# First feed-forward layer of an attention and MLP kernel: a second Strassen level for two of the seven products, by pairs of steps

## The chip, the cores and the metric

The kernel runs on one core of one Trainium2 chip. The metric is the device time of one execution in microseconds (us). Three runs of the kernel before gave 872.02, 872.38 and 872.67; the median is 872.38.

The engines are called as the profile calls them: PE (TensorE) multiplies matrices and writes to PSUM, which has eight banks of 128x512 float32; PEld is PE's loading of weights; DVE (VectorE), ACT (ScalarE) and POOL (GpSimd) work elementwise; SP (SyncE) issues the DMAs.

## The reference

Attention in which a query sees only the keys of its own hash bucket, then an MLP with a fast GELU, all in float32 (the weights of the MLP come as float64):

```python
q_bits = (np.einsum('bhsd,dk->bhsk', q, proj) > 0)          # 6 bits a row, the bucket
mask = q_bucket[:, :, :, None] == k_bucket[:, :, None, :]
attn = softmax(where(mask, q @ k.T / 8, -1e9)); x = attn @ v # B, H, S, D = 4, 8, 768, 64
h = x @ w_in                                                 # x: 3072 x 512, w_in: 512 x 2048
g = h * (1.0 / (1.0 + np.exp(-1.702 * h)))
out = g @ w_out                                              # w_out: 2048 x 512
```

## The kernel before

**Stages.** Attention goes over 16 pairs of heads and leaves `xT`, x transposed, in SBUF (to 316 us of the profile). `feed_forward` (line 695) computes h in a first layer (316.6 to 606.2 us) and out in a second (to 866). Both layers use Strassen's scheme in Winograd's form: a product of two matrices, each cut into 2x2 quarters, is made with seven products of quarters or of sums of quarters, in place of eight. `sums_a` (line 208) makes the four sums of a left matrix, `sums_b` (line 216) those of a right one. The dictionaries `LEFT` and `RIGHT` say which quarter or sum each of the products 1 to 7 takes.

**The first layer.** It has 24 steps, numbered 0 to 23: three blocks of 1024 tokens (`sb`), eight pieces of w_in's columns (`mt`) in each. A step is one call of `hidden` (line 731): seven products of 128x512, each two matmuls over the inner dimension (`product`, line 716). A product goes to a PSUM bank; products 6, 7 and 4 are added up in the bank of product 1 (`start=False`), product 3 in that of product 5. ACT copies the bank between them to `u`, `v` and `c22` in SBUF (lines 726, 746, 750), DVE adds the bank of product 5 to c22 (line 751), product 2 to u (line 755), product 3's bank to v (line 764), ACT applies the GELU in place (line 741). So a step ends with four quarters of g. POOL then makes the sums of these quarters that the second layer wants (lines 219 to 222, "POOL's four" below), and SP stores quarters and sums in DRAM (line 738). The first product of the next step stands ahead of products 4 and 3 (`head`).

**What else runs in the first layer.** The order on PE, DVE, ACT and POOL is the order in which the program is written (`ORDERED`, line 18, under `tc.manual_schedule`); SP's order is the scheduler's. At the ends of the steps DVE gets, from the dictionary `todo` (lines 917 to 929):

- the conversions of w_out's 16 chunks and of the last two of w_in from float64 (`convert`, line 158: lines 180, 182, 188, 193, 195 and 198 on DVE, line 190 on ACT, line 162 the DMA of the chunk `raw`), one chunk in a step, with one buffer for `raw`; none in steps 0, 7 and 15;
- the four x sums of the next token block (`sums_b` on 128x1024) in steps 7 and 15: three before products 4 and 3, one after;
- sums of w_out (`low` from step 17, `high` in step 21), and sums of g at the end.

POOL gets the sums of w_in for the next step in the first eight steps (`in_sums`, line 236), later some of w_out (`inner_sums`). When step 0 has been written, attention writes its last part: `invert` and `norm` (lines 488 and 504) divide the last heads by their sums, on DVE. In step 21 the pool of the conversions is closed, and `fetch(0)` (line 802) brings the first quarter of g for the second layer.

**PSUM.** Six banks for the products, two for the conversions (`part`, `size`). The tiles u, v, c12, c21 and c22 have two buffers each.

Of the kernel before, what the change touches and what calls it, by code (L numbers as in the profile page):

```python
# [19 lines left out]
P = 128  # L20
# [18 lines left out]
def kernel(  # L39
# [168 lines left out]
    def sums_a(eng, a11, a12, s3, a22, s1, s2, s4, a21=None):  # L208

        a21 = s3 if a21 is None else a21  # L210
        return [lambda: eng.tensor_tensor(s1, a21, a22, op=Alu.add),
                lambda: eng.tensor_tensor(s3, a11, a21, op=Alu.subtract),
                lambda: eng.tensor_tensor(s2, s1, a11, op=Alu.subtract),
                lambda: eng.tensor_tensor(s4, a12, s2, op=Alu.subtract)]

    def sums_b(eng, b11, b12, b21, b22, t1, t2, t4):


        return [lambda: eng.tensor_tensor(t1, b12, b11, op=Alu.subtract),  # L219
                lambda: eng.tensor_tensor(b12, b22, b12, op=Alu.subtract),  # L220
                lambda: eng.tensor_tensor(t2, b22, t1, op=Alu.subtract),  # L221
                lambda: eng.tensor_tensor(t4, b21, t2, op=Alu.subtract)]
# [4 lines left out]
    def quarters_in(cols):  # L227
        w = [w_in_sb[:, K2 * k : K2 * (k + 1), F2 * i + cols.start : F2 * i + cols.stop]
             for i in range(2) for k in range(2)]
        return w + [s_in[:, i, :, cols] for i in range(3)]  # L230
# [2 lines left out]
        x = [xT[:, K2 * k : K2 * (k + 1), (2 * sb + j) * XT : (2 * sb + j + 1) * XT] for k in range(2) for j in range(2)]  # L233
        return x + [t_x[:, i] for i in range(3)]

    def in_sums(mt):
        return sums_a(nc.gpsimd, *quarters_in(slice(mt * P, (mt + 1) * P)))


    def load(ld, n, v_bufs=2):  # L240
# [454 lines left out]
    def feed_forward(tag, late=()):  # L695
# [9 lines left out]
        with ExitStack() as fctx:  # L705
            stage_ctx = fctx.enter_context(ExitStack())
            stage = stage_ctx.enter_context(tc.tile_pool(name=f"stage{tag}", bufs=2, side="right"))
            late = list(late)
            sets = [fctx.enter_context(tc.tile_pool(name=f"f0{tag}", bufs=6, space=PSUM, side="right"))]
            todo, turn = {}, [-1]  # L710

            def bank():
                turn[0] += 1
                return sets[turn[0] % 8 // 6 if len(sets) > 1 else 0].tile([P, XT], F32, tag="p", name="product")

            def product(ps, sb, mt, i, start=True):
                wq, xq = quarters_in(slice(mt * P, (mt + 1) * P)), quarters_x(sb)
                for kc in range(K2):
                    nc.tensor.matmul(ps, wq[LEFT[i]][:, kc, :], xq[RIGHT[i]][:, kc, :],  # L719
                                     start=(start and kc == 0), stop=(kc == K2 - 1), skip_group_check=not start)  # L720

            def head(n):

                ps, u = bank(), stage.tile([P, XT], F32, tag="u", name="u")
                product(ps, *divmod(n, FC // 2), 1)
                nc.scalar.copy(u, ps)  # L726
                return ps, u

            heads = {}

            def hidden(sb, mt, mid=(), end=()):
                n = sb * (FC // 2) + mt
                a, u = heads.pop(n) if n in heads else head(n)
                v, c12, c21, c22 = (stage.tile([P, XT], F32, tag=x, name=x) for x in ("v", "c12", "c21", "c22"))
                t2, t4 = (stage.tile([P, XT], F32, tag=x, name=x, bufs=1) for x in ("t2", "t4"))

                def keep(at, x):
                    loader[0].dma_start(out=g_dram[len(LEFT) * sb + at, :, mt, :], in_=x)

                def emit(c, at=None, of=None):  # L740
                    nc.scalar.activation(c, c if of is None else of, Act.Gelu_apprx_sigmoid)  # L741
                    if at is not None:
                        keep(at, c)

                product(a, sb, mt, 6, False)
                nc.scalar.copy(v, a)
                b = bank()
                product(b, sb, mt, 5)
                product(a, sb, mt, 7, False)
                nc.scalar.copy(c22, a)  # L750
                nc.vector.tensor_tensor(c22, b, c22, op=Alu.add)
                emit(c22, 3)
                c = bank()
                product(c, sb, mt, 2)
                nc.vector.tensor_tensor(u, c, u, op=Alu.add)
                emit(u, 0)
                if n + 1 < n1 * (FC // 2):
                    heads[n + 1] = head(n + 1)
                for x in mid:
                    x()  # L760
                product(a, sb, mt, 4, False)
                emit(c21, 2, a)
                product(b, sb, mt, 3, False)
                nc.vector.tensor_tensor(c12, b, v, op=Alu.add)  # L764
                emit(c12)

                for f, kept in zip(sums_b(nc.gpsimd, u, c12, c21, c22, v, t2, t4), ((4, v), (1, c12), (5, t2), (6, t4))):
                    f()
                    keep(*kept)
                for x in end:  # L770
                    x()

# [29 lines left out]
            def fetch(n):  # L802
                sb, o = steps_out[n]
                for h in range(2):
                    cs = slice(h * F4, (h + 1) * F4)
                    loader[0].dma_start(out=raw_g[n % 2][:, cs], in_=g_dram[len(LEFT) * sb + RIGHT[o], :, cs, :])
# [90 lines left out]
                            yield  # L897
                    yield

            MT = FC // 2  # L900
            for sb in range(n1):
                for mt in range(MT):
                    n = sb * MT + mt
                    if n == 1:
                        wop = fctx.enter_context(tc.tile_pool(name=f"wo{tag}", bufs=1))
                        cv_ctx = fctx.enter_context(ExitStack())
                        cv = cv_ctx.enter_context(tc.tile_pool(name=f"cv{tag}", bufs=1))
                        cps = cv_ctx.enter_context(tc.tile_pool(name=f"cps{tag}", bufs=1, space=PSUM))


                        w_out_sb = wop.tile([P, 4, FC, P], F32, name="w_out_sb")
                        wqs += [w_out_sb[:, 2 * i : 2 * i + 2, MT * k : MT * (k + 1), :] for i in range(2) for k in range(2)]
                        wqs += [xT[:, i, 0 : 4 * XT].rearrange("p (h c d) -> p h c d", h=2, d=P) for i in range(3)]

                        order = [8 * k + 4 * c + i for c in range(2) for k in range(2) for i in range(4)]
                        chunks = [(w_out_sb[:, :, fc, :].rearrange("p r x -> p x r"), wo[fc]) for fc in order]
                        steps = conversions(cv, cps, late + chunks)
                        free = [i for i in range(LATE + 1, 3 * MT) if i % MT != MT - 1]
                        for i in (list(range(1, LATE + 1)) if late else []) + free[:FC]:
                            todo[i] = [lambda: next(steps)] * 2  # L920
                        low, high = (sums_a(nc.vector, *(x[:, :, F4 * c : F4 * (c + 1), :] for x in wqs)) for c in range(2))
                        first = 2 * MT + 1
                        for i, f in enumerate(low):
                            todo[first + i] = todo[first + i] + [f]
                        todo[first + 1] = todo[first + 1] + inner_sums(0)[:2]
                        todo[first + 2] = todo[first + 2] + inner_sums(0)[2:]
                        todo[first + 4] = high + inner_sums(1)
                        todo[first + 5] = inner_sums(2)
                        todo[first + 6] = inner_sums(3)
                    if n == 3 * MT - 3:  # L930
                        cv_ctx.close()
                        sets.append(fctx.enter_context(tc.tile_pool(name=f"f1{tag}", bufs=2, space=PSUM)))
                        turn[0] = 7
                        gp = fctx.enter_context(tc.tile_pool(name=f"gp{tag}", bufs=1))
                        raw_g[0] = gp.tile([P, FC // 2, XT], F32, name="raw_g")
                        fetch(0)
                    if sb == 0 and mt + 1 < MT:
                        for f in in_sums(mt + 1):
                            f()
                    x = sums_b(nc.vector, *quarters_x(sb + 1)) if mt == MT - 1 and sb + 1 < n1 else []  # L940
                    t = {3 * MT - 2: g_sums(0)[:2], 3 * MT - 1: g_sums(0)[2:]}.get(n, []) if n > 3 * MT - 3 else []
                    hidden(sb, mt, x[:3] + ([lambda: fetch(1)] if n == 3 * MT - 1 else []), x[3:] + t + todo.pop(n, []))
                    yield
            stage_ctx.close()
            st2 = fctx.enter_context(tc.tile_pool(name=f"st2{tag}", bufs=1, side="right"))
            ys.update({j: st2.tile([P, XT // 32, P], F32, name=f"y{j}") for j in range(2)})
# [105 lines left out]
```

## Time and profile before

| | |
|---|---|
| median of 3 runs | 872.38 us |
| the profiled execution | 872.87 us |
| its span, first to last instruction | 871.0 us |
| mean granted TensorE clock | 0.997 |
| PE, DVE, POOL busy in 316.6 to 606.2 | 288.79, 171.58, 156.61 us of 289.6 |
| the same in 606.2 to 866 | 254.40, 213.24, 38.02 us of 259.8 |

A row of the profile's groups names the line, the engine, the operation, the tile written and those read, the shape and the count; after the bar come the busy time in us, the mean of one in ns, and the idle time of the engine before them with what ended it. A row of the timeline has the start in us, the duration (of the whole run of instructions, where "x3" says that three are merged), engine, line, operation, and in brackets the idle time before it. A row of the waits has the waiting instruction, what released it, the us in total, how many times, and the longest. A float32 matmul leaves two records in the trace.

### The profile page before, as it was taken

The numbers are of one execution on the slowest core, as the hardware profiler recorded it, in microseconds if no ns is written. First come the engines' busy times: TensorE is split into PE (matmuls) and PEld (weight loads), VectorE is DVE, ScalarE is ACT, GpSimd is POOL, SyncE is SP. The second block draws the span as 40 slices with busy tenths as digits, with TensorE's granted clock in tenths as the row PEclk, the third lists the DMA queues.
The fourth block names the chain that finished last, engine by engine and source line by source line (L and its number), as shares of the span: only waits on it lengthen the run. The fifth ranks groups of instructions, "written<-read, shape, count | busy, mean of one in ns | idle before, by whom it ended". The sixth has DMA issues, their size and how long they took to land.

```text
span 871.0 us, 13350 instructions
## 1 busy us (share of the span) xinstructions
PE 857.9 (99%) x4845; PEld 499.2 (57%) x4845; DVE 661.4 (76%) x924; ACT 340.2 (39%) x567; POOL 311.6 (36%) x275
## 2 busy tenths in 40 slices
PE   9999999999999999999999999999999999999996
PEld 5444444444444444444444444445878888888885
DVE  4589999999999875457555556676788977897786
ACT  5866667776666643434334333433000000000000
POOL 4242234333223465665443344559903100000000
PEclk9999999999999999999999999999999999999998
DMA  5636645456652104665456655576744675467524
GB/s 127 96 57 109 104 84 85 84 99 117 99 97 61 56 2 157 205 208 181 172 198 197 217 181 172 190 254 223 271 156 158 199 243 201 163 209 243 194 97 99
DMA packets 169161, 132.09 MB, mean 152 GB/s; under 512 B 123616, under 2 KB 138112, under 8 KB 163712
## 3 DMA queue, kind: packets, MB, share of 16 engines
q1 hardware_dynamic: 166528, 129.70, 52.5%
q10 hardware_dynamic: 2560, 1.46, 0.8%
q8 instruction: 40, 0.66, 0.3%
q14 instruction: 33, 0.27, 0.1%
HBM read 79.69 MB, written 50.33 MB: 149 GB/s over the span
## 4 chain that ended last, share of the span: by engine, by line
PE 95%; DVE 3%; issue 0%; DMA 0%; ACT 0%; ACTq 0%; DVEq 0%
PE product L719 33%; PE product L851 26%; PE ps L432 18%; PE av L465 15%; DVE xT L855 1%; PE dn L486 1%; PE hash L408 1%; PE tp L366 1%; DVE y L831 1%; DMA k<-in_k_dram 0%; DVE v L855 0%; PE hash L373 0%; DVE t2a L221 0%; DVE raw_g L220 0%; ACTq L838 0%
## 5 line engine op out<-in xcount | busy, mean ns | idle before, releaser
L433 ACT ACTIVATE e<-ps 128x768 f32<-128x768 f32 x192 | 151.2, 812 | 25.7 <-PE ps L432 23.2
L432 PE MATMUL ps<-qT,kT 64*128 64x384 f32 x768 | 155.1, 482 | 0.0
L465 PE MATMUL av<-e,v 128*32 128x385 f32 x1536 | 128.0, 487 | 0.0
L719 PE MATMUL product<-xT,w_in_sb 128*128 128x512 f32 x288 | 127.8, 592 | 0.0
L440 POOL TENSOR_TENSOR acc<-e 128x768 f32<-128x768 f32 x32 | 51.7, 1617 | 194.4 <-ACT e L433 175.0
L719 PEld LDWEIGHTS product<-xT,w_in_sb 128*128 128x128 f32 x288 | 54.6, 190 | 69.0 <-issue 68.5
L465 PEld LDWEIGHTS av<-e,v 128*32 128x32 f32 x1536 | 48.6, 109 | 76.2 <-issue 74.9
L432 PEld LDWEIGHTS ps<-qT,kT 64*128 64x128 f32 x768 | 68.0, 187 | 38.5 <-issue 38.4
L719 PE MATMUL product<-t_x,s_in 128*128 128x512 f32 x192 | 86.4, 592 | 0.8 <-ACT u L726 0.8
L764 DVE TENSOR_TENSOR c<-product,v 128x512 f32<-128x512 f32 x24 | 16.6, 690 | 90.8 <-PE product L719 90.8
L219 POOL TENSOR_TENSOR v<-c,u 128x512 f32<-128x512 f32 x24 | 32.3, 1345 | 128.1 <-ACT c L741 128.1
L864 ACT COPY u<-product 128x256 f32<-128x256 f32 x21 | 7.8, 372 | 174.1 <-PE product L851 140.9
L719 PEld LDWEIGHTS product<-t_x,s_in 128*128 128x128 f32 x192 | 36.4, 190 | 47.1 <-issue 45.2
L432 PE MATMUL ps<-qf,kf 64*128 64x384 bf16 x384 | 62.9, 324 | 0.1
L741 ACT ACTIVATE c<-c 128x512 f32<-128x512 f32 x48 | 30.3, 630 | 72.3 <-DVE c L764 43.7
L441 POOL TENSOR_TENSOR acc<-acc,e 128x768 f32<-128x768 f32 x32 | 55.8, 1745 | 2.5
L446 DVE SCALAR_TENSOR_TENSOR acc<-e 128x768 f32<-128x768 f32 x32 | 47.7, 1489 | 5.1 <-ACT e L433 5.1
L719 PE MATMUL product<-t_x,w_in_sb 128*128 128x512 f32 x96 | 45.1, 592 | 0.0
L719 PE MATMUL product<-xT,s_in 128*128 128x512 f32 x96 | 45.1, 592 | 0.0
L750 ACT COPY c<-product 128x512 f32<-128x512 f32 x24 | 14.1, 586 | 66.3 <-PE product L719 66.3
L432 PEld LDWEIGHTS <-kf 64*128 64x128 bf16 x384 | 18.9, 94 | 35.1 <-issue 6.2
L448 DVE TENSOR_TENSOR acc<-acc,e 128x768 f32<-128x768 f32 x32 | 34.3, 1071 | 3.3
(206 smaller groups left out, 1513.4 us busy)
## 6 DMA issues: line engine op xcount, KB each, us to landing
raw_g<-g_dram SPq DMA_DIRECT2D x22, 1024.0 KB
s_in<-g_dram SPq DMA_DIRECT2D x20, 1024.0 KB
g_dram<-c SPq DMA_DIRECT2D x72, 256.0 KB
g_dram<-t SPq DMA_DIRECT2D x48, 256.0 KB
raw<-in_moe_w_in_dram SPq DMA_DIRECT2D x16, 512.0 KB
raw<-in_moe_w_out_dram SPq DMA_DIRECT2D x16, 512.0 KB
v<-in_v_dram SPq DMA_DIRECT2D x32, 192.0 KB
g_dram<-u SPq DMA_DIRECT2D x24, 256.0 KB
```

Of the source, the lines that this page charges most:

```text
L219: return [lambda: eng.tensor_tensor(t1, b12, b11, op=Alu.subtract), lambda: eng.tensor_tensor(b12, b22, b12, op=Alu.subtract), lambda: eng ...
L432: nc.tensor.matmul(ps[:, j, 0:HS], a[hs, keys], m[hs, cols], start=not last, stop=last)
L433: nc.scalar.activation(es[c][:, kt, :, 0:HS], ps[:, :, 0:HS], Act.Exp, scale=1.0 / D**0.5)
L440: nc.gpsimd.tensor_tensor(acc, es[c][:, 0, :, 0:HS], es[c][:, 1, :, 0:HS], op=Alu.add)
L441: nc.gpsimd.tensor_tensor(acc, acc, es[c][:, 2, :, 0:HS], op=Alu.add)
L446: nc.vector.scalar_tensor_tensor(acc, e[0], T * TINY, e[1], op0=Alu.add, op1=Alu.add)
L448: nc.vector.tensor_tensor(acc, acc, x, op=Alu.add)
L465: nc.tensor.matmul(av[D * j + d : D * j + d + 32, :], vt[:, t, j, d : d + 32], es[c][:, t, j, :], start=(t == 0), stop=(t == T - 1))
L719: nc.tensor.matmul(ps, wq[LEFT[i]][:, kc, :], xq[RIGHT[i]][:, kc, :], start=(start and kc == 0), stop=(kc == K2 - 1), skip_group_check=not ...
L741: nc.scalar.activation(c, c if of is None else of, Act.Gelu_apprx_sigmoid)
L764: nc.vector.tensor_tensor(c12, b, v, op=Alu.add)
L851: nc.tensor.matmul(ps, wq[LEFT[i]][:, c, :], gq[RIGHT[i]][:, c, :], start=(c == 0), stop=(c == F4 - 1))
```

## The change

Ten pairs of steps (numbered 0 to 9, steps 0 to 19) replace ten times two calls of `hidden`; steps 20 to 23 stay single. In a pair, product 2 over both steps, and product 3 over both, is seen as one product of a left matrix of 256x256 and a right one of 256x512, and is made with seven matmuls of 128x256 (`nested`) in place of eight column halves, which were four matmuls of 128x512. The seven go in six parts: part 1 is matmul 1, part 2 matmuls 6 and 2, parts 3 to 6 matmuls 7, 5, 4 and 3. Matmuls 1, 6, 7 and 4 are added up in one PSUM bank ("a"), 2, 5 and 3 go to another ("x"); the pool `inner` has one buffer of each. After each matmul DVE adds the bank so far to a 128x256 half of u or v. The parts of product 2 (S1 to S6 below) stand between the other products of the pair, those of product 3 (T1 to T6) behind the last one and between the products of the next pair (`behind`).

```python
def nested(o, sb, t, base, done):
    (q11, q12), (q21, q22) = ((x[:, 0:TH], x[:, TH:XT]) for x in base)
    ...
    def first():
        add(q11, go(1, "a"), q11)
    def second():
        add(q12, go(6), q12)
        add(q11, go(2, "x"), q11)
    def third():
        add(q22, go(7), q22)
    def fourth():
        add(q22, go(5, "x"), q22)
    def fifth():
        add(q21, go(4), q21)
        done(1)
    def sixth():
        add(q12, go(3), q12)
        done(0)
```

The order of a pair (`old()` is the next part of product 3 of the pair before; `hook(i)` is other work, put in below):

```python
p1(0); old(); hook(1); p1(1); old()
yield
hook(2); p6(0); old(); hook(3); p6(1); old(); hook(4); p5(0); old()
second = nested(2, sb, t, u, done2)
second[0](); hook(5); p7(0); corner(0); second[1](); hook(6); p7(1); second[2]()
hook(7); p5(1); corner(1); second[3](); hook(8); p4(0); second[4]()
hook(9); p4(1); second[5]()
third = nested(3, sb, t, v, done3)
third[0](); behind.extend(third[1:]); hook(10)
```

`p5` adds product 5's bank to v at once, `corner` adds it to c22. POOL's four, now for both steps, eight sums of 128x512, are written after T6 (`done3`). At the `yield` in pair 0 attention writes `invert` and `norm`; before, they came after the whole of step 0.

The nested products need sums of their own: `nest_w` makes eight of 128x128 on POOL for a pair's weights (pairs 0 to 3, kept for the later token blocks), `nest_x` eight of 128x256 on DVE for a token block (pairs 0, 4 and 8). The hooks:

```diff
+                if t == 0:
...
+                    more = nest_x(0, places[0])
+                    hooks[3] = more[2] + nest_w(0)
+                    hooks[4] = more[3]
...
+                if at == 0 and sb > 0:
+                    on(1, more[2])
+                    on(3, more[3][:2])
+                    on(4, more[3][2:])
+                x = todo.pop(2 * t, [])
+                on(2, x[0:1])
+                on(3, x[1:2])
+                on(5, x[2:])
+                x = todo.pop(2 * t + 1, [])
+                on(7, x[0:1])
+                on(9, x[1:2])
+                on(10, x[2:])
+                if t + 1 < MT // 2:
+                    on(5, in_sums(t + 1))
+                    on(8, nest_w(t + 1))
+                if at == MT // 2 - 1:
+                    x = sums_b(nc.vector, *quarters_x(sb + 1))
+                    more = nest_x(sb + 1, places[sb + 1])
+                    on(8, x[0:1])
+                    on(9, x[1:2])
+                    on(10, x[2:4])
```

So a chunk's conversion, before in one go at the end of a step, is cut in two: lines 180, 182 and 188 at hook 2 or 7, lines 193, 195 and 198 at hook 3 or 9. `in_sums` now makes the sums of two steps at once (128x2x256). The four x sums stand at hooks 8, 9 and 10 of pairs 3 and 7, the eight of `nest_x` in pairs 4 and 8 at hooks 1, 3 and 4.

Buffers: PSUM has four banks for the products of a pair, two for the nested ones, two for the conversions. u, v and c22 have four buffers and c21 three (two in the pool `stage`, the others in a pool `twice`, which lies where attention's small tiles were); t1, t2 and t4 have one. v is no longer overwritten by a sum; the sum has t1. In step 21 `twice` and `inner` are closed with the pool of the conversions, before `fetch(0)`.

## The prediction

> **What bounds the kernel now.** I read the page first: busy time, then the chain that ended last.
>
> ```profile
> PE 857.9 (99%) x4845; PEld 499.2 (57%) x4845; DVE 661.4 (76%) x924; ACT 340.2 (39%) x567; POOL 311.6 (36%) x275
> ...
> PE 95%; DVE 3%; issue 0%; DMA 0%; ACT 0%; ACTq 0%; DVEq 0%
> ```
>
> TensorE (PE) sets the time. The chain in order of time gives the rate of each stage.
>
> ```profile
> 319.38 286.92 PE product L719 x668
> ...
> 686.08 160.83 PE product L851 x744
> ```
>
> In the first layer (316.6 to 606.2 us) 668 records take 286.92 us, 429.5 ns each; a matmul of 128x512 leaves two records (672 for 336), so one product (two matmuls) takes 1.718 us. A record of 256 columns, each with weights of its own, takes 160.83/744 = 216.2 ns: a nested matmul takes 0.432 us. The waits, filtered to PE, show how little of the first layer is idle now.
>
> ```profile
> PE product L851 <- DVE t2a L221: 1.7, 1, 1.7
> ...
> PE product L719 <- ACT u L726: 0.8, 1, 0.8
> ```
>
> So nothing is won by moving work off other engines, only by fewer PE columns; and every new wait of PE is paid in full.
>
> **What is removed.** A product over two steps took 2 x 1.718 = 3.436 us; nested it takes 7 x 0.432 = 3.027. Twenty products save 20 x 0.409 = **8.2 us**. The first step's wait of 0.8 goes too, because two first products now stand there. What is late next is VectorE (DVE).
>
> **What DVE gets.** Its timeline in one step (start, duration):
>
> ```profile
> 403.78 0.69 DVE L764 TENSOR_TENSOR c<-product,v 128x512 f32<-128x512 f32 x1 [4.46 <-PE product L719]
> 404.38 0.68 DVE L180 TENSOR_SCALAR part<-raw 128x512 uint32<-128x512 uint32 x1
> 405.10 0.69 DVE L182 SCALAR_TENSOR_TENSOR bits<-raw,part 128x512 uint32<-128x512 uint32 x1
> 405.83 0.69 DVE L188 TENSOR_SCALAR part<-bits 128x512 uint32<-128x512 uint32 x1
> 406.55 0.70 DVE L193 SCALAR_TENSOR_TENSOR part<-raw,part 128x512 f32<-128x512 uint32 x1
> 407.29 1.05 DVE L195 TENSOR_TENSOR w_out_sb<-bits,part 128x512 f32<-128x512 f32 x1
> 408.44 1.05 DVE L198 SCALAR_TENSOR_TENSOR w_out_sb<-size,w_out_sb 128x512 f32<-128x512 f32 x1
> ```
>
> From start to start a 512 add costs 0.60; the first half of a conversion 2.1 (L180, L182, L188), the second 2.9 (L193, L195, L198). A 256 add from PSUM has a row of its own below, 0.41; pairs of them follow at 0.37. A nested pair gives DVE 14 x 0.37 + 4 x 0.60 + 2 x 5.0 = 17.6 us in 23.2 us of PE: it fits on average. But DVE is in order, and each nested chain has one PSUM bank: part 6 or 7 may not write until DVE has added the part before. On PE a pair runs p1, T2, p1, T3, p6, T4, p6, T5, p5, T6, S1, p7, S2, p7, S3, p5, S4, p4, S5, p4, S6, T1 (S: second product, T: third, of which five parts hang over into the next pair). S1 comes at 11.2 us of the pair and takes the bank that DVE empties with T5's add. DVE: T3's add ends at 5.4, half a conversion 7.5, T4's add 7.8, the other half 10.7, T5's add 11.1, and PE starts 0.15 after DVE (637.37 after 637.22 in the trace): 11.2. **The slack is zero**; whatever makes DVE later in the first half of a pair is paid by PE one to one. Behind a waiting S1 stand all later products. Four things make it later.
>
> *The start.* Now DVE normalises the last heads after the whole first step; the changed order puts that, and the eight sums of the x blocks (128x256), ahead of the first add.
>
> ```profile
> 332.29 0.57 DVE L492 STREAM_TRANSPOSE rt<-dn 128x384 f32<-128x384 f32 x1
> ...
> 335.20 1.33 DVE L506 TENSOR_TENSOR xT<-xT,rs 128x768 f32<-128x768 f32 x1
> ```
>
> That is 4.2 us. DVE is busy with L178 to L222 until 323.05, so norm ends at 327.3, eight sums at 0.45 (0.44 apart at 642.36, below) at 331.0, the first 512 add and S1's add at 332.1. PE reaches S2 after five products, S1 and p7: 316.6 + 8.6 + 0.4 + 1.7 = 327.3. Wait **5.0**. Low end 2.5 (L178 to L198 took 1.1 beside POOL, 0.69 elsewhere); high end 9, eight sums beside POOL at about 1.0:
>
> ```profile
> 627.52 1.07 DVE L855 TENSOR_TENSOR v<-v,xT 128x256 f32<-128x256 f32 x1
> ...
> 642.36 0.88 DVE L855 TENSOR_TENSOR xT<-xT 128x256 f32<-128x256 f32 x2
> ```
>
> I take 5.0, the nearer row. The first of these has POOL (GpSimd) busy beside it, the second not.
>
> *The turns of the x blocks (pairs 4 and 8).* Four sums of 128x1024 now fall at the end of pairs 3 and 7 and after T1; then eight of 128x256 in the next pair, before T5's add. At 1.22 each (411.25 to 416.4, POOL idle) S1 waits 1.9; all at 2.17 (598.53, POOL at 2.25 beside it) about 5.1. POOL's eight sums of a pair (1.35 us each) begin after T6 and last to the end of the pair, so about half meets them. I take **3.0 each, 6.0** (3.8 to 10.2).
>
> The Trainium skill (SBUF — State Buffer, "Who interferes with whom") states that a DVE instruction with two SBUF inputs contends with a GpSimd instruction that reads SBUF, one with at most one SBUF input does not. The trace agrees: L751 (one input in PSUM) stays at 0.69 beside L220 at 601.9. By that rule the nested adds stay at 0.41 and the x sums do not; the sum would be nearer the high end of the two terms above.
>
> *The loader.* A raw chunk has one buffer, and its DMA stands behind other stores on SP.
>
> ```profile
> 409.09 1.67 SPq L738 DMA_DIRECT2D g_dram<-t  x2
> 410.87 0.37 SPq L162 DMA_DIRECT2D raw<-in_moe_w_out_dram  x1
> ```
>
> In the changed order the chunk for a pair's first conversion is issued after POOL's last store of the pair before and three held-back stores, at about 1.6 us of the pair; DVE wants it at 5.4. At 339.48 such a DMA was issued, and L180 read at 344.30 without waiting: it takes at most 4.8, so it may be up to 1 us late, with three stores of 0.65 us ahead perhaps 1.5. Pairs 2, 3, 5, 6, 7, 9: 0 to 9 us; I take **2.7**.
>
> *The rest.* POOL's sums of w_in for the next pair follow its eight: p6 may wait 0.7 twice, I take 0.7 (0 to 3). Wide w_out sums of 2.1 us in pairs 8 and 9: 0.5 (0 to 2). In steps 20 to 23, single again, the c22 and v copies wait on ACT behind the last T parts: 1.0 (0 to 1.5).
>
> **Sum.** -8.2 - 0.8 + 5.0 + 6.0 + 2.7 + 0.7 + 0.5 + 1.0 = +6.9. The profiled execution took 872.87 (span 871.0), 0.5 over the median of the runs: 872.4 + 6.9 = about **879.5 us**. The ends: all low -2.7 (869.7), all high about +26.
>
> One row could overturn the gain itself; the row of the 256 adds stands below it.
>
> ```profile
> L851 PE MATMUL product<-raw_g,xT 128*128 128x256 f32 x152 | 35.1, 379 | 0.0
> ...
> L855 DVE TENSOR_TENSOR xT<-product,xT 128x256 f32<-128x256 f32 x45 | 17.4, 413 | 0.0
> ```
>
> The 379 is a record from start to modelled end. If it were its share of PE, nested parts would cost more than they replace; but 744 records in 160.83 us exclude that. The order of the changed kernel does show 140 small matmuls in place of 80 large ones, so it does what it says.
>
> **Rivals.**
> 1. *DVE keeps ahead; faster.* Place: S1 in each pair. If the chunk always lands before 5.4 us, the x sums miss POOL's and the start costs 2.5, waits come to 6.3 against 9.0 saved: 869.7, 869.5 as a round figure. It decides at waits of 9. For it: DVE's idle time now, 24% of the span. Against: the start alone is fixed by 4.2 us of norm. 0.13.
> 2. *It cancels*, waits of 7.5 to 11: 872.4. 0.10.
> 3. *The loader falls behind everywhere*: 9 in place of 2.7: 886, up to 893 with POOL contention. For it: every store now waits in SP behind POOL's eight. 0.15.
> 4. *The clock drops after the long waits.* The granted clock reads 1.00 over each of the two layers (stretches 316.6 to 606.2 and on to 866), which hold the waits of 0.8 and 1.7; a wait of 5 has no row. If half the clock were granted as long as the wait lasted, +2.5 at the start and about 1.3 in each of pairs 4 and 8: 884.5. 0.07. The Trainium skill (TensorE: Matmul & The Clock Gate, "What's actually happening") has the clock halved after an idle window of about 3.4 us; by that rule this rival acts at the start alone.
> 5. The forecast, 874.1 to 886: 0.55.
>
> **The numbers.** A measurement here tells about 0.2% (1.7 us) from no change. Faster 0.13 (rival 1), same 0.10 (rival 2), slower 0.55 + 0.15 + 0.07 = 0.77. The range 870.5 to 888 leaves out most of rival 1 and the upper half of rival 3, 0.2 together.
>
> **What would show it.** PE's waits in the first layer name DVE at the nested line: one of 4 to 6 us about 11 to 16 us after the first product, two of 2 to 4 us a third and two thirds on, and about 0.5 in other pairs. PE's busy time falls by about 8. L180 waits for a DMA if the loader term is real. Wrong if PE shows fewer than 9 us of waits, or if S2's first wait is under 2.5.

## The result, and the profile after

The changed kernel takes 891.94 us (median of 4 executions, 890.42 to 892.73) against 872.2 for the kernel before in the same comparison: ratio 1.0224, 95% interval 1.0206 to 1.0242. It is 19.7 us slower. The forecast was 7.1 us slower than 872.4, with a range up to 888.0: the direction was right, the size was not.

The page of the changed kernel, PE's and DVE's busy time and the shares of the chain that ended last:

```profile
PE 858.9 (97%) x4965; PEld 522.4 (59%) x4965; DVE 705.7 (79%) x1068; ACT 340.5 (38%) x567; POOL 324.5 (36%) x291
...
PE 74%; DVE 13%; POOL 4%; issue 4%; DMA 3%; ACT 1%; SPq 0%; ACTq 0%; DVEq 0%; POOLq 0%
```

PE holds 74% of the chain, where it held 95% before: DVE, POOL and a DMA are now on it. PE's busy time should have fallen by 8 and has risen by 1. So part of the loss is not waiting at all: PE was busy for longer with less work. The chain in order of time says which stage lost it.

```profile
589.25 35.69 PE product L739 x76
624.94 20.73 PE product L1056 x96
...
704.71 160.83 PE product L1056 x744
```

In the chain, the second layer (line 1056, line 851 before) starts at 624.94, in the kernel before at 606.30: 18.6 us later. Its long piece of 744 records takes 160.83 us as before. The spans of the two profiled executions differ by 18.5 us (889.5 and 871.0), so all of the loss is in the first layer. PE's waits there:

```profile
PE small L800 <- DVE v L749: 9.1, 9, 2.0
PE small L800 <- issue: 5.2, 1, 5.2
PE product L739 <- DVE w_out_sb L198: 4.1, 1, 4.1
```

Line 800 is the nested matmul, line 749 DVE's add behind it. The 5.2 is S2's wait at the start. The row says "issue" because the release that ended it is not in the records, but DVE is at work until S1's add ends, and S2 starts right behind it (DVE, then PE):

```profile
332.51 0.41 DVE L749 TENSOR_TENSOR u<-small,u 128x256 f32<-128x256 f32 x1
...
333.02 1.19 PE L800 MATMUL small<-w_out_sb,w 128*128 128x256 f32 x2 [5.16 <-issue]
```

The 4.1 was in no step of the prediction. Together 18.4 us, against which stand 9 of saving: some 9 are still missing.

Most of these are in the clock. The timeline of PE around the third wait (start, duration, count):

```profile
583.30 1.88 PE L739 MATMUL product<-t_x,s_in 128*128 128x512 f32 x4
589.25 3.78 PE L739 MATMUL product<-t_x,s_in 128*128 128x512 f32 x4 [4.07 <-DVE w_out_sb L198]
```

The same four records take 1.88 us before the wait and 3.78 behind it. The windows of the start (start and end in us, length, busy us of PE, PEld, DVE, ACT and POOL with counts, granted clock, DMA share, GB/s) show the same:

```profile
328.00:330.00 2.00, 0.00 (x0) 0.00 (x0) 2.00 (x4) 1.76 (x2) 1.84 (x5) 1.00 0.68 205
...
332.00:334.00 2.00, 0.98 (x2) 0.83 (x3) 1.52 (x3) 0.45 (x1) 1.92 (x3) 0.53 0.00 0
334.00:336.00 2.00, 2.00 (x5) 1.30 (x4) 0.85 (x2) 0.18 (x1) 2.00 (x2) 0.50 0.35 131
336.00:338.00 2.00, 2.00 (x3) 0.72 (x3) 0.00 (x0) 0.00 (x0) 1.84 (x4) 0.50 0.00 0
338.00:340.00 2.00, 2.00 (x6) 1.14 (x5) 0.77 (x2) 1.15 (x2) 1.84 (x5) 0.77 0.00 0
```

The granted clock falls to 0.50 as PE's wait ends. The trace's clock records have two such stretches in the first layer, each 6.83 us long: one behind the wait at the start, one behind the wait at 589.25. PE still stood for the first 0.92 us of one and the first 1.15 of the other; the rest, at half clock, cost it about 3.0 and 2.8 us. The other 4 us or so are spread over the pairs.

Now every pair can be weighed. Ten products at 1.718 us and fourteen nested matmuls at 0.432 make 23.23 us; pair 0 lacks T2 to T6 (2.59), the part from step 20 on has them besides four steps. What each took above that, from the starts of the pairs' first products in the traces, in us (the versions below the first are experiments, told next):

| | 0 | 1 | 2 | 3 | 4 | 5 | 6 | 7 | 8 | 9 | 20 to 23 | sum |
|---|---|---|---|---|---|---|---|---|---|---|---|---|
| changed kernel | 8.8 | 0.0 | 1.3 | 1.0 | 1.8 | 1.8 | 0.9 | 0.9 | 1.8 | 2.2 | 7.4 | 27.9 |
| e3_queue | 9.4 | 0.5 | 0.1 | 0.4 | 1.9 | 0.0 | 0.0 | 0.0 | 1.9 | 0.0 | 6.2 | 20.4 |
| e9_first | 2.5 | 0.0 | 0.1 | 0.0 | 1.9 | 0.0 | 0.0 | 0.0 | 1.9 | 0.0 | 0.4 | 6.8 |
| e10_xpool | 2.5 | 0.0 | 0.0 | 0.1 | 0.8 | 0.0 | 0.0 | 0.0 | 0.8 | 0.0 | 0.4 | 4.6 |

The products alone are 9.2 us shorter than the first layer before (280.4 against 289.6, its first step's wait included); 27.9 - 9.2 = 18.7.

### The profile page after: what moved, and what is told of

Its sections match the earlier page's. It is cut to its first block, busy times and chain, and to the rows that moved or that the text cites. A ratio compares the mean times of both kernels' runs of the same rounds, so it can differ in the third digit from the quotient of the medians.

```text
span 889.5 us, 13736 instructions
## 1 busy us (share of the span) xinstructions
PE 858.9 (97%) x4965; PEld 522.4 (59%) x4965; DVE 705.7 (79%) x1068; ACT 340.5 (38%) x567; POOL 324.5 (36%) x291
## 4 chain that ended last, share of the span: by engine, by line
PE 74%; DVE 13%; POOL 4%; issue 4%; DMA 3%; ACT 1%; SPq 0%; ACTq 0%; DVEq 0%; POOLq 0%
PE product L1056 26%; PE ps L432 17%; PE av L465 13%; PE product L739 12%; PE small L800 3%; DMA raw<-in_moe_w_out_dram 3%; DVE xT L1060 1%; DVE v L749 1%; PE dn L486 1%; PE hash L408 1%; DVE w_out_sb L195 1%; POOL t L222 1%; POOL t L221 1%; POOL t L219 1%; DVE bits L182 1%
## 5 line engine op out<-in xcount | busy, mean ns | idle before, releaser
L739 PE MATMUL product<-xT,w_in_sb 128*128 128x512 f32 x208 | 99.7, 607 | 0.0
L739 PE MATMUL product<-t_x,s_in 128*128 128x512 f32 x192 | 91.5, 603 | 4.2 <-DVE w_out_sb L198 4.1
L219 POOL TENSOR_TENSOR t<-v,u 128x512 f32<-128x512 f32 x24 | 33.3, 1386 | 125.3 <-ACT v L746 125.3
L739 PEld LDWEIGHTS product<-xT,w_in_sb 128*128 128x128 f32 x208 | 40.6, 196 | 33.8 <-issue 31.5
L749 DVE TENSOR_TENSOR v<-small,v 128x256 f32<-128x256 f32 x70 | 28.9, 418 | 24.3 <-PE small L800 24.3
L749 DVE TENSOR_TENSOR u<-small,u 128x256 f32<-128x256 f32 x70 | 28.5, 417 | 16.3 <-PE small L800 8.0
L448 DVE TENSOR_TENSOR acc<-acc,acc 128x768 f32<-128x768 f32 x32 | 31.7, 991 | 6.3 <-POOL acc L441 3.2
L1056 PE MATMUL product<-raw_g,xT 128*128 128x256 f32 x152 | 35.1, 379 | 0.0
```

Source lines behind the costliest of these rows:

```text
L448: nc.vector.tensor_tensor(acc, acc, x, op=Alu.add)
L749: nc.vector.tensor_tensor(dst, x, y, op=Alu.add)
L1056: nc.tensor.matmul(ps, wq[LEFT[i]][:, c, :], gq[RIGHT[i]][:, c, :], start=(c == 0), stop=(c == F4 - 1))
```

## The experiments

The theory: three separate costs that the sum had missed or had too small. At the start and in step 21, a long wait is followed by half clock; in step 21, a PSUM bank that DVE frees late; in pairs 2 to 9, the transfer of `raw`, late because it stands behind the stores of g in SP's order. The rivals: the clock drops come of their own; DVE is late by its own work, and the waits stay when their releaser is mended. All ratios are to the kernel before on the same chip, where it took 872.2 to 872.8.

**e1_bank.** Product 5 of step 21 takes its bank from the pool that lies where `part` and `size` of the conversions were, and step 20's conversion ends on DVE at 589.2. One line gives it the nested products' banks:

```diff
-                return (outer if at < 4 else sets[at // 2 - 2]).tile(...)
+                return (outer if at < 4 else sets[3 - at // 2]).tile(...)
```

> Only the order of the two late PSUM pools is turned round, so that step 21's fifth product takes the bank that the nested products left instead of the one of the last conversion. Theory: the 4.07 us wait at 589.25 goes, and with it the 6.83 us at half clock that stand right behind it (3.4 us of PE's time): 891.9 - 4.1 - 3.4 = 884.4. Rival 'the half clock comes of its own, not of the wait': 891.9 - 4.1 = 887.8, with two stretches of half clock still in the record. Rival 'DVE is late there anyway, and the wait moves to the next product': 891 to 892.

Measured: 886.47 us (883.23 to 886.81), ratio 1.0160 (1.0143 to 1.0177). PE around the place:

```profile
580.56 1.88 PE L739 MATMUL product<-xT,s_in 128*128 128x512 f32 x4
582.27 3.60 PE L739 MATMUL product<-t_x,s_in 128*128 128x512 f32 x8
585.73 4.56 PE L739 MATMUL product<-xT,w_in_sb 128*128 128x512 f32 x10
```

No wait, eight records in 3.60 us, granted clock 1.00 in all windows from 572 to 588: the wait and the half clock behind it went together, so the second did not come of its own. The last part took 0.7 over its products, after 7.4. The profiled execution, 883.2, agrees with the theory; the three others were some 3.3 us longer, and the one trace does not show why. Half clock alone is not the reason: their mean granted clocks were 0.991, 0.994 and 0.994, against 0.993.

**e4_warm and e8_warm12.** Both fill the start's wait with products of zeros; nothing else is changed.

```diff
+                if t == 0:
+                    x = inner.tile([P, XT], F32, tag="x", name="warm")
+                    for _ in range(22):          # 12 in e8_warm12
+                        nc.tensor.matmul(x, idle[:, 0:P], idle, start=True, stop=True)
                 second[1]()
```

> 22 products of zeros into a free PSUM bank are put into the stretch at the start in which PE waits for the x sums; nothing else moves. Theory: PE does not stand idle there, the 6.83 us at half clock behind it do not come, and the kernel gains their half though no wait is shorter: 891.9 - 3.4 = 888.5 (889 to 890 if the zeros run past the x sums). Rival 'the half clock does not hang on PE's being idle': 891.9 to 893.

Measured: 888.10 (887.75 to 888.95), ratio 1.0181 (1.0164 to 1.0198): 3.8 us less than the changed kernel, with work added and no product earlier. The window that stood at 0.50:

```profile
334.00:336.00 2.00, 2.00 (x7) 1.05 (x6) 0.28 (x2) 0.61 (x2) 1.92 (x3) 1.00 0.35 131
```

So the clock drop hangs on PE's being idle, and its price at the start is 3 to 4 us: 3.8 by the medians, 2.9 by the first pair, which is 5.9 us over its products in this trace, after 8.8.

> As the run with 22 products of zeros at the start, with 12: they run for about 2.6 us and PE then still stands idle for about 2.7 us before S2. In the runs so far waits of 3.4, 4.1 and 5.2 us were followed by half clock and waits up to 2.2 us were not. If it is the length of the idle time: no half clock, 888 to 889 as with 22. If it is that PE is idle at all in such a stretch: half clock, 891.5 to 892.5.

Measured: 889.78 (889.22 to 892.23), ratio 1.0196 (1.0179 to 1.0213): between the two. PE's timeline at the start and in the last nested pair:

```profile
327.31 2.75 PE L906 MATMUL warm<-idle 128*128 128x512 bf16 x12
332.64 1.19 PE L800 MATMUL small<-w_out_sb,w 128*128 128x256 f32 x2 [2.58 <-issue]
...
553.76 0.97 PE L800 MATMUL small<-xT,w_in_sb 128*128 128x256 f32 x2 [2.42 <-DVE v L749]
554.53 3.35 PE L739 MATMUL product<-xT,w_in_sb 128*128 128x512 f32 x4
```

A wait of 2.58 us, and one of 2.42 in pair 9, were each followed by half clock, but for 3.41 us, half as long. Both expectations missed: it is neither the whole price nor none. In pair 9 the changed kernel's wait was 2.0 and cost no clock; the wait of 2.42 and the clock behind it made that pair 2.4 us longer here. The profiled execution, 892.2, is the slowest of the four by as much; whether the others were spared this drop is not shown.

The clock records tell more of the condition. In each trace, the changes of the clock lie on a grid of 3.413 us: the two stretches of the changed kernel start at 332.10 and 588.10, which is 75 times 3.413 apart. From trace to trace the grid lies elsewhere. What counts is how long PE stands within one window of this grid. Over the 13 traces, each of the 12 windows at full clock in which PE stood for 2.1 us or more was followed by half clock; where it stood for 1.67 us or less, none was; in between, one of ten. A window at half clock was followed by a second one where PE stood for 0.9 us or more in it (9 of 9), and by full clock where it stood for less than 0.5 (13 of 13). So the length of the wait alone does not decide: 2.42 us within one window (here, pair 9) brought half clock, and 2.19 us that the grid cut into 1.33 and 0.86 (e5_start2, pair 9) brought none.

**e2_start and e5_start2.** The first pair alone is laid out otherwise: S2 to S6 one product later, and product 3's four x sums later on DVE (e2_start) or on POOL (e5_start2).

```diff
-                    hooks[4] = more[3]
+                    hooks[7] = more[3]           # e2_start; in e5_start2 hook 4, on nc.gpsimd
...
-                second[1]()
+                if t > 0:
+                    second.pop(0)()
```

> The first pair alone is laid out otherwise: the four x sums of product 3 come later (behind the seventh product of its second step), and S2 to S6 each one product later. Theory: S2 then finds its x sums about 1.3 us late instead of 5.2, and a wait so short is not followed by half clock: 891.9 - 3.9 - 3.4 = 884.6. Rival 'the half clock comes of its own': 888.0 with the stretch still there. Rival 'S2 waits for POOL's weight sums and not for DVE': 891 to 892.

Measured: 893.09 (889.90 to 895.53), ratio 1.0232 (1.0200 to 1.0264): no gain. S2's wait fell to 1.07, about as expected (it was now for POOL's sums of weights), but a new one came. DVE, then PE:

```profile
331.78 1.23 DVE L783 TENSOR_TENSOR w_out_sb<-xT 128x256 f32<-128x256 f32 x1
333.04 1.37 DVE L784 TENSOR_TENSOR w_out_sb<-xT,w_out_sb 128x256 f32<-128x256 f32 x1
334.33 1.48 DVE L785 TENSOR_TENSOR w_out_sb<-xT 128x256 f32<-128x256 f32 x1
335.74 1.48 DVE L786 TENSOR_TENSOR w_out_sb<-xT,w_out_sb 128x256 f32<-128x256 f32 x1
```

```profile
340.85 1.22 PE L800 MATMUL small<-w_out_sb,w_in_sb 128*128 128x256 f32 x2 [3.43 <-DVE u L749]
```

Moved, the four sums met POOL's sums of w_in (128x512) and took 5.4 us in place of 2.4. S5 then waited 3.43 us for DVE, and 6.83 us of half clock followed. The move traded one wait for another.

> The start of the first pair again: S2 to S6 one product later as before, but product 3's four x sums on GpSimd, behind its sums of weights, instead of later on VectorE, where they took 5.4 us beside GpSimd's sums and pushed S5 back by 3.4. Theory: S2 waits about 1.1 us as it did there, S5 does not wait over 1 us, no half clock follows: 891.9 - 4.1 - 3.4 + 0.5 = 885 (884 to 886). Rival 'VectorE has too much to do in the first pair in any order': a wait over 3 us stands at S5 or S6, half clock follows it, 889 to 893. Rival 'GpSimd is then late with the second pair's weight sums': the wait stands in the second pair, 888 to 891.

Measured: 888.47 (886.01 to 890.66), ratio 1.0191 (1.0173 to 1.0209). In its trace the first pair is 2.5 us over its products, after 8.8, with no half clock there; S2's wait is 1.07, and T1, right behind S6, waited 0.39. So the start cost 6.3 us more than it had to. The median is 3.5 us better, less than those 6.3; the profiled execution, 886.0, is the lowest of the four, and what the others lost is again not in a trace. The two slowest, 889.3 and 890.7, had a lower mean granted clock, 0.991 and 0.990 against 0.993, which is worth 2 to 3 us; it fits a further stretch of half clock, but does not show one.

**e3_queue.** ACT issues the w_out transfers, right behind the read (line 193) that frees the buffer.

```diff
-                gens = [convert(cv, *x, psum=psum) for x in chunks]
+                gens = [convert(cv, *x, queue=nc.scalar, psum=psum) for x in chunks]
...
-                    for y in gens[i + 1 : i + 2]:
-                        next(y)
                     for at, _ in enumerate(x):
                         if at == 2:
                             yield
+                        if at == 3:
+                            for y in gens[i + 1 : i + 2]:
+                                next(y)
```

In the changed kernel, in pair 5 (from 442.9), the buffer was free at 441.58. SP's timeline, and DVE's:

```profile
442.13 1.67 SPq L743 DMA_DIRECT2D g_dram<-t  x2
443.89 1.38 SPq L743 DMA_DIRECT2D g_dram<-c  x3
445.36 0.51 SPq L162 DMA_DIRECT2D raw<-in_moe_w_out_dram  x1
```

```profile
450.17 0.70 DVE L180 TENSOR_SCALAR part<-raw 128x512 uint32<-128x512 uint32 x1 [1.89 <-DMA raw<-in_moe_w_out_dram]
```

The transfer stood 3.8 us behind five stores of g, the first two of which waited for POOL; DVE stood 1.89 for it, and S1 in this pair 1.56 for DVE.

> The transfers of the w_out chunks are issued by ScalarE, behind the read that frees their only buffer, instead of standing in SP's order behind the stores of g. Theory: pairs 2 to 9 of the changed kernel are 0.9 to 2.2 us longer than their products, 11.7 us together, because L180 waits for the transfer (six waits of 1.4 us on VectorE); with the transfer there 3 us earlier those waits go and most of the 11.7 us with them: 891.9 - 9 = 883 (880.5 to 885). Rival 'VectorE is late by its own work in those pairs (the x sums, the conversion's two halves)': the waits of L180 go and PE's stay, 890.5 to 892. Rival 'ScalarE's order suffers, its copies are late': slower than 892.

Measured: 883.33 (882.63 to 885.04), ratio 1.0128 (1.0111 to 1.0146): 8.6 us less. In the experiment's trace, ACT issues the same chunk and L180 reads it:

```profile
440.24 0.33 ACTq L162 DMA_DIRECT2D raw<-in_moe_w_out_dram  x1
```

```profile
446.78 0.68 DVE L180 TENSOR_SCALAR part<-raw 128x512 uint32<-128x512 uint32 x1
```

No wait; the table's second row has pairs 2, 3, 5, 6, 7 and 9 within 0.4 of their products. Not all of the gain is the transfers': by the table 6.9 us of it lie in pairs 1 to 9, and 1.2 in the last part, where the wait of 4.07 us was followed by 3.41 us of half clock in place of 6.83. (It had stood for 2.92 us in one window of the grid and 1.15 in the next; here it ended before its second window did.) The rival, DVE late by its own work, holds in pairs 4 and 8 alone.

**e6_three.** The mends of e1_bank, e3_queue and e5_start2 together.

> The three mends together: the late banks turned round, the w_out chunks issued by ScalarE, the first pair laid out as in the run before. Theory: the three costs are separate and add up, 891.9 - 7.0 (start) - 7 (bank, by its own run 5.5 to 8.7) - 8.6 (transfers) = 869.3 (867 to 872). That is the 9 us that product 2 and the start gave (872.2 - 9.0 = 863.2) and some 6 us still lost: 1.9 in each of the two turns of an x block, 1.4 in the first pair, 1 in the second to fourth. Rival 'the costs overlap, one mend uncovers the next': 874 to 880.

Measured: 876.23 (874.66 to 877.52), ratio 1.0048 (1.0031 to 1.0064): the costs add up but for 7 us. In the first pair ACT issued the first chunk at 330.18, behind an activation that waited for DVE, and DVE stood for it:

```profile
334.62 0.69 DVE L180 TENSOR_SCALAR part<-raw 128x512 uint32<-128x512 uint32 x1 [3.41 <-DMA raw<-in_moe_w_in_dram]
```

S5, and T1 right behind S6, waited 1.6 and 1.7 us for DVE behind it. Besides, the time from the last product to the end was 11.0 us, against 8.9 in the kernel before: 2.1 of the 7. It was 10.8 in e9_first and 9.0 in e10_xpool; why is not settled.

**e7_three_x.** As e6_three, with product 3's x sums in pairs 4 and 8 later on DVE:

```diff
-                    on(3, more[3][:2])
-                    on(4, more[3][2:])
+                    on(6, more[3][:2])
+                    on(8, more[3][2:])
```

> As the run before, and in the two pairs in which an x block turns (the fifth and the ninth) product 3's four x sums go from ahead of the sixth and fifth products to behind the fifth's adds, since they are wanted only in the next pair. Theory: of the 1.9 us by which each of these pairs was longer than its products, 1.5 is a wait of the nested products behind those sums; it goes: 3 us less than the run before, 866 (864.5 to 869). Rival 'the sums cost VectorE the same wherever they stand': as the run before within 0.7.

Measured: 880.32 (878.20 to 882.48), ratio 1.0089 (1.0065 to 1.0112): 4 us slower than e6_three. In pair 4 three of the four sums now lie beside POOL's sums of g; two of them, and the add behind them:

```profile
430.45 1.34 DVE L784 TENSOR_TENSOR xT<-xT 128x256 f32<-128x256 f32 x1
431.83 1.38 DVE L785 TENSOR_TENSOR xT<-xT 128x256 f32<-128x256 f32 x1
433.13 0.41 DVE L749 TENSOR_TENSOR u<-small,u 128x256 f32<-128x256 f32 x1
```

These two took 1.34 and 1.38 (0.42 at their old place), the nested add, which reads PSUM, 0.41. T1 waited 1.34 and pair 5 began late: 2.8 and 1.3 us over their products, where it was 1.9 and 0.0. Both theories missed: the sums cost more where they were put. The trace has, besides, 3.41 us of half clock in the first pair, which the trace of e6_three has not.

**e9_first and e10_xpool.** e9_first is e6_three with the first chunk issued by SP again; e10_xpool has, besides, the eight x sums of pairs 4 and 8 on POOL, which stood idle there for 13.5 us (e6_three).

```diff
-                gens = [convert(cv, *x, queue=nc.scalar, psum=psum) for x in chunks]
+                gens = [convert(cv, *x, queue=nc.scalar if i else None, psum=psum) for i, x in enumerate(chunks)]
...
-                    eng = nc.gpsimd if (o, sb) == (3, 0) else nc.vector
+                    eng = nc.vector if (o, sb) == (2, 0) else nc.gpsimd    # e10_xpool
```

> As the run of the three mends together (876.2), but the first chunk's transfer is issued by SP again; ScalarE issues those behind it. There ScalarE issued the first one only behind a corner's activation, at 330.2 us, it landed 4.4 us later, VectorE stood 3.4 us at L180 for it and two waits of 1.7 us of S5 and S6 followed in the first pair. Theory: these two go, 876.2 - 3.3 = 873 (872 to 875). Rival 'the transfers by ScalarE cost something of their own': 875.5 to 877.5.

Measured: 871.57 (870.58 to 874.20), ratio 0.9989 (0.9980 to 0.9999): level with the kernel before.

> As e9_first, and the eight x sums of 128x256 in the fifth and the ninth pair on GpSimd, which stands idle for 13.5 us there, instead of VectorE. Theory: VectorE gets 3.3 us back in each of these pairs, the wait of 1.5 us there goes and with it nearly all of the 1.95 by which the two pairs were longer: 3 to 3.9 us less than e9_first, 869.5, faster than the kernel before by 0.3%. Rival 'the four big x sums alone (7 us on VectorE) already make that wait': 1 us less at most. Rival 'GpSimd's sums slow VectorE's down and S2 waits for GpSimd': the same as e9_first or slower.

Measured: 868.45 (867.32 to 868.72), ratio 0.9951 (0.9938 to 0.9965): the fastest, 4.4 us under the kernel before and 23.5 under the changed one. All waits of PE over 1.3 us in the two layers:

```profile
PE product L1058 <- DVE t2a L221: 1.7, 1, 1.7
```

which is the wait that the kernel before had in its second layer. The nested products' waits are 1.1 (POOL), 1.1 and 0.4 us in all. The eight sums were 1.15 of the 1.95 in each turn; in the other 0.8 stands a wait of 0.55 for the add behind the four sums of 128x1024.

**e11_bank_warm.** The edits of e1_bank and e4_warm together.

> The turned banks of e1_bank and the 22 products of zeros of e4_warm in one kernel: no stretch of half clock is left in the first layer, while the start's wait of 5.2 us and the transfers' waits stay. e1_bank's profiled execution took 883.2, its three others 886.4 to 886.8, and its one trace shows no cause for that. Theory: the two half-clock costs are separate, 883.2 - 3.8 = 879.4, up to 883 where the unknown 3.3 us come too. If the unknown 3.3 us are a stretch of half clock in another pair (the last nested one, where a wait of 2.4 us was followed by one in e8_warm12), the executions fall in two groups again. Rival 'the two overlap, one stretch is had in any case': 886.

Measured: 882.05 (881.28 to 883.33), ratio 1.0106 (1.0089 to 1.0123). The granted clock is 1.00 all through the first layer. It is 9.9 us under the changed kernel. In the trace the first pair is 2.9 us shorter than in the changed kernel, the last part 6.9, the wait of 4.1 and 2.8 behind it: both half-clock costs are there to be had, one beside the other. The four executions lie within 2.1 us.

## Why the prediction was wrong, point by point

| term of the sum | forecast | measured in the changed kernel |
|---|---|---|
| products 2 and 3, and the first step's wait | -9.0 | -9.2 |
| the start | +5.0 | +5.9 (e4_warm, first pair), and 2.9 of half clock |
| the turns of the x blocks | +6.0 | +3.9 (e9_first, pairs 4 and 8) |
| the loader | +2.7 | +7.8 (11.7 over pairs 1 to 9, less 3.9; 6.9 of it went in e3_queue) |
| w_in's and w_out's sums, single steps | +2.2 | about 0.4 (e9_first, the last part) |
| step 21's bank, and half clock behind it | not seen | +4.1 and about 3 |
| sum | +6.9 | +18.7 |

Without the half clock and step 21 the measured terms come to +8.8, near the forecast. That is in part luck: the loader was 5.1 dearer than its term, the turns and the small sums 3.9 cheaper.

- **The saving** was right: a nested pair whose parts do not wait takes 23.21 us (pair 1), where two steps took 24.03. So was "the slack is zero": S1 is the part that waits in pairs 2 to 9, for T5's add.
- **The start.** The wait was right (5.0 against 5.2), for the reason given, but two errors offset each other: the eight sums took 4.6 us and not 3.7, most of them at 0.67 each beside POOL's sums of weights, and PE came to S2 some 0.4 us later than worked out. What failed is that the clock drop of rival 4, at 0.07, was kept out of the sum. The clock was halved for 6.83 us behind a wait of 5.2, not "as long as the wait lasted"; the price, 2.9 us, was close to the rival's 2.5. The rival placed it in pairs 4 and 8 too, where waits of 1.3 brought none.
- **The step that failed outright** is "in steps 20 to 23, single again ... 1.0". It counted copies on ACT and not the banks: before, step 21 went on in banks that the products had, and the conversions' two were reached later; now its product 5 takes one of these two at once, and step 20's conversion, 5 us of DVE, ends at 589.2. The wait of 4.1 and the half clock behind it are 7 of the 12 us by which the sum was short; the loader adds 5 and the start 4, and the terms that were too dear take 4 off.
- **The loader** was mis-sized: 2.7 for 7.8, in reach of its high end of 9. The mechanism was the one named, a chunk behind POOL's last store and held-back stores on SP. In pair 5 it was issued 2.5 us into the pair, not 1.6, and landed 4.8 later, 1.9 late, not 1 to 1.5. It was late in six pairs, and paid by S1 nearly in full.
- **The turns** were too dear, 3.0 for 1.9 each: the four big sums took 1.22 to 1.95 us each (e6_three, pairs 3 and 4), and the eight small ones 0.42, since POOL's four had not begun. The terms for w_in's and w_out's sums were not seen at all.
- **The rivals.** Rival 1, DVE keeps ahead, gave 869.5 on the ground of 24% idle DVE; e10_xpool is that kernel in effect, 868.45, but only with DVE's work and the transfers laid out for it. Rival 3 came true at 7.8 of its 9.

The Trainium skill (TensorE: Matmul & The Clock Gate, "What's actually happening") has a free-running window of 3413 ns, and the halved clock after at least one idle window of about 3.4 us. The length agrees: all stretches of half clock in the first layer were 3.41 or 6.83 us; and so does the free run, by the grid told under e8_warm12. The condition does not: 2.1 us of standing in one window was always enough, and once 1.69 us was (e7_three_x, first pair), while nine windows with 1.69 to 1.87 us brought none. The measurement decides: here a wait of 2.1 us is already at risk, if it falls into one window.

What stays open: what decides between 1.67 and 2.1 us; what parts the executions of e1_bank and e5_start2 by 3 to 5 us; and the 2 us at the end of e6_three and e9_first.

## What to carry to other kernels

When a change makes PE wait, price the wait and then look for what the granted clock does behind it: here two waits of 4 and 5 us cost some 6 us more than they lasted. When tiles change pools, follow each PSUM bank and each DMA queue past the edit to its next user, at the end of the loop too: the two largest misses, the bank of step 21 and the transfer of `raw`, came about that way. And work that is moved off a busy spot should be checked against what the other engines do at the new one: the same sum on DVE took 0.42 us at one place and 1.3 to 1.5 beside POOL.

## What the runs showed of the hardware that was not expected

- The granted clock went to exactly 0.5 in stretches of 3.41 or 6.83 us. Its changes lie on a grid of 3.413 us: 2.1 us of PE's standing within one window of it brought half clock in the next, in 12 of 12 cases, and 0.9 us in that one a second, in 9 of 9. The same wait of 4.07 us brought one such window or two, as it fell on the grid.
- A 128x256 sum on DVE with both inputs in SBUF took 0.42 us alone and 1.23 to 1.52 us beside POOL's sums of 128x512; an add of the same size with one input in PSUM stayed at 0.41 (e7_three_x, 433.13). The Trainium skill (SBUF — State Buffer, "Who interferes with whom") has the two engines lock one shared pair of ports against each other; the trace agrees, with the numbers just given.
- A mended wait can give back more than it lasted: e1_bank's wait was 4.1 us, and its last part got 6.7 us shorter.
